# Range checks in halves behind the score transposes, reduced one step later, in an attention and two-layer FFN kernel

## The chip, the cores and the metric

The kernel runs on one core of a Trainium2 chip. The metric is the device time of one execution in microseconds (us). Before the change it is 730.16 us, the median of three runs (728.69 to 731.04).

The engines go by short names: PE is TensorE (PEld its weight loads), DVE VectorE, ACT ScalarE, POOL GpSimd, SP the engine that issues nearly all DMAs here. Each works through its own instructions in order and waits on semaphores for the others.

## What is computed

Attention over 4 batches, 8 heads, 768 positions and 64 dimensions, with a few global keys (`n_global` 8) and a local causal window (`n_local` 96), followed by two matrix products with an activation between them:

```python
scores = scale * np.matmul(q, k.transpose(0, 1, 3, 2)) + bias   # bias: -slope * distance
scores = np.where(keep, scores, -1000000000.0)                  # keep: global or local
a = np.exp(scores - np.max(scores, axis=-1, keepdims=True))
a = a / (np.sum(a, axis=-1, keepdims=True) + 1e-09)
x = np.matmul(a, v)                  # then heads side by side: 3072 tokens x 512
h = x @ w_in                         # 512 x 2048
g = np.where(h >= 1, h, np.where(h <= -1, 0.0, (h + 1) ** 2 / 4.0))
out = g @ w_out                      # 2048 x 512
```

q, k and v are float32; the two weight matrices arrive as float64.

## The kernel before

The 3072 tokens are 24 units of 128 (`UNITS`: batch and block; the first blocks of the four batches come first), and 12 chunks of two units. A unit's eight heads are handled in two halves of four. A half-unit n = 2 * unit + half goes through two functions:

- `attend`: score matmuls `s` (L295) into PSUM; on DVE bias and minimum (`z`, `nm`, L304); exponentials on ACT (L310); the probabilities `ph` as a float16 high part (ACT, L364) and low part (DVE, L365); and a DMA transpose `pt` of both, issued by SP (L369).
- `attend2`: output products `av` of `pt` with the values `vt` (L395); on DVE the division by the sum, giving `x` (L401); high and low parts `xh` (ACT L404, POOL L405); and a second DMA transpose, `xt` (L409).

The first block of a batch has versions without DMA transposes.

The FFN of a chunk is 8 calls of `ffn1` (24 matmuls L467, then ACT L475, DVE L479 and L480, ACT L483, POOL L484) and 8 of `ffn2` (12 matmuls each, L498). High and low parts of weights and activations take the place of float32 matmuls. `load` brings a unit's q, k and v; `load_v` (L246) loads a block of values into `vr`, a ring of three buffers, and splits it into `vt` on ACT (L214) and DVE (L216). `weight` loads and splits one 128-wide piece of a weight matrix.

The kernel is valid only for inputs within certain ranges. It therefore collects range data on the way, compares them at the end (L139 to L147, result `badi`), and takes a general path if a limit is broken. For this it reads inputs a second time:

- `check_weight(num, src)`, 32 of them: a 512 KB load of a weight piece into `c_raw` (L437), in the ring `stage` of three buffers, then two reduces on DVE (L443), largest and least magnitude, of 128 x 512 elements each.
- `check_qkv(num)`, 12 of them: a 512 KB load of values (`cqkv`, L277), then on ACT a square with an accumulated sum (L278).

The order is written by hand as a list of slots. A slot is one `ffn1` call or one `ffn2` call, and 16 slots make a chunk. Half-unit n's `attend` is traced at slot `first[n]` (4n - 16 - `LEAD`, so 4n - 23, from n = 12 on) and its `attend2` at `second[n]`, that is `first[n] + GAP`, at most `first[n + 2]`, and before its own chunk's slot; the loads `LDGAP` slots ahead of `attend`. From chunk `CK0` = 4 on, the checks are spread evenly over the slots up to the middle of chunk 11, weights first. A planner then lays out each engine's instructions: among those that are ready by its model of durations, the one traced first goes first. `tc.issue_after(ins)` makes what is traced under it, and runs on the engine of `ins`, come after `ins` in that engine's order; it adds no wait.

```python
        while c >= CK0 and checks and len(checks) > NCK - NCK * (slot + 1 - 16 * CK0) / (16 * (11.5 - CK0)):
            f, args = checks.pop(0)
            with tc.issue_after(late[-1].ins):
                f(*args)
```

`late` holds the `xt` transposes, which SP issues. So a check's load comes behind the latest `xt` on SP, and the reduces are placed by the planner alone.

## Time and profile before

| what | value |
|---|---|
| median of three runs | 730.16 us (728.69 to 731.04) |
| the profiled execution, its own time | 727.93 us |
| its span, first to last instruction | 726.2 us |
| DMA traffic | 97.40 MB, mean 134 GB/s |
| DVE reduces of the checks | 64 |
| squares of the value checks on ACT | 12 |

The profile is one execution. The page gives busy time, share of the span and number of instructions of each engine, then the chain of work that ended last, by line. Other views list waits (who waited for whom), a timeline (start, length, engine, line, operation, tiles, and in brackets the idle time before it and what ended it), groups of equal instructions, and busy time in chosen stretches. Matmuls overlap, so one lasts longer than the distance to the next. "SPq" is an instruction of SP's queue; for a DMA its length is the time to issue it, not to land.

### The profile page before, as it was taken

To read this page: it belongs to the slowest core of one execution; us is meant where nothing else is said; L and a number is where in the kernel's file an instruction comes from. 1 tells how busy PE (TensorE), PEld (TensorE's weight loads), DVE (VectorE), ACT (ScalarE), POOL (GpSimd) and SP (SyncE) were. 2 spreads that over 40 slices of the span, in tenths; PEclk is the share of its full clock that TensorE was granted. 3 is DMA by queue.
4 is the path that set the end of the run, shared out by engine and by line. 5 is a ranking of instruction groups with operands and counts; after the bars stand their busy time and mean duration, and the time that the engine had idled before them with its cause. 6 is when DMAs were issued, how large, how long until landed. Compare 5 with 4: busy or idle time off the path is not lost.

```text
span 726.2 us, 13000 instructions
## 1 busy us (share of the span) xinstructions
PE 647.0 (89%) x4912; PEld 434.0 (60%) x4912; DVE 418.5 (58%) x1023; ACT 358.4 (49%) x906; POOL 203.4 (28%) x200
## 2 busy tenths in 40 slices
PE   1787699999899999899997899898899799799995
PEld 1575577656756857646745755663674674475762
DVE  2678899764744744745843863654583674272240
ACT  1575578854634735524733553443552463473530
POOL 0222467432411422311420421240231141042130
PEclk9999799999999999999999899899899999999998
DMA  7544655567434456576466547546366445645301
GB/s 256 185 146 143 207 187 176 121 143 159 96 80 111 113 102 140 119 149 173 121 164 181 120 111 169 143 106 164 97 182 147 112 110 117 138 95 132 115 2 34
DMA packets 161191, 97.40 MB, mean 134 GB/s; under 512 B 116576, under 2 KB 145248, under 8 KB 161120
## 3 DMA queue, kind: packets, MB, share of 16 engines
q1 hardware_dynamic: 160256, 95.44, 51.7%
q10 hardware_dynamic: 864, 1.05, 0.4%
q8 instruction: 40, 0.66, 0.4%
q14 instruction: 31, 0.25, 0.1%
HBM read 63.97 MB, written 6.29 MB: 97 GB/s over the span
## 4 chain that ended last, share of the span: by engine, by line
PE 57%; DMA 15%; DVE 9%; issue 8%; ACT 4%; SPq 3%; POOL 3%; DVEq 0%; POOLq 0%; ACTq 0%
PE o L498 25%; PE h L467 22%; DMA pt<-ph 6%; PE s L295 5%; DMA c_raw<-in_moe_w_in_dram 4%; PE av L395 3%; DMA c_raw<-in_moe_w_out_dram 3%; ACT z L310 2%; POOL xh L405 2%; DVE sq L443 2%; SPq L409 1%; DVE w L479 1%; SPq L369 1%; DMA w_raw<-in_moe_w_in_dram 1%; DVE w L480 1%
## 5 line engine op out<-in xcount | busy, mean ns | idle before, releaser
L467 PE MATMUL h<-xt,wih 128*128 128x256 f16 x1536 | 267.2, 280 | 4.7 <-DVE w L479 4.7
L467 PE MATMUL h<-xt,wil 128*128 128x256 f16 x768 | 214.7, 280 | 0.0
L484 POOL TENSOR_TENSOR gl<-w,gh 128x512 f16<-128x512 f32 x96 | 121.4, 1270 | 239.4 <-ACT gh L483 230.9
L467 PEld LDWEIGHTS <-wih 128*128 128x128 f16 x1536 | 152.0, 100 | 37.1 <-issue 13.1
L310 ACT ACTIVATE z<-z,nm 128x256 f32<-128x256 f32 (+1 forms) x192 | 91.8, 479 | 139.1 <-DVE nm L304 139.1
L498 PE MATMUL o<-woh,gh 128*128 128x512 f16 x384 | 149.3, 389 | 1.4 <-ACT gh L483 1.4
L498 PE MATMUL o<-wol,gh 128*128 128x512 f16 x384 | 148.8, 388 | 0.0
L498 PE MATMUL o<-woh,gl 128*128 128x512 f16 x384 | 147.4, 387 | 0.0
L498 PEld LDWEIGHTS <-gh 128*128 128x128 f16 x768 | 74.1, 99 | 88.5 <-issue 11.1
L483 ACT ACTIVATE gh<-w 128x512 f16<-128x512 f32 x96 | 60.2, 627 | 92.6 <-DVE w L480 91.9
L479 DVE SCALAR_TENSOR_TENSOR w<-h,u 128x512 f32<-128x512 f32 x96 | 65.7, 684 | 54.6 <-ACT u L475 50.7
L443 DVE TENSOR_REDUCE sq<-c_raw 128x1 f32<-128x512 f32 x64 | 40.9, 680 | 86.1 <-DMA c_raw<-in_moe_w_in_dram 44.1
L304 DVE CUSTOM_DVE_ANT_0 z<-s,bias 128x256 f32<-128x256 f32 (+1 forms) x192 | 67.0, 395 | 34.3 <-PE s L295 34.1
L467 PEld LDWEIGHTS <-wil 128*128 128x128 f16 x768 | 77.1, 100 | 11.4 <-POOL wil L224 0.3
L475 ACT ACTIVATE u<-h,half 128x512 f32<-128x512 f32 x96 | 64.7, 674 | 26.3 <-PE h L467 26.2
L405 POOL TENSOR_TENSOR xh<-x,xh 128x256 f16<-128x256 f32 x40 | 36.9, 922 | 137.1 <-ACT xh L404 136.1
L480 DVE SCALAR_TENSOR_TENSOR w<-u,w 128x512 f32<-128x512 f32 x96 | 72.6, 756 | 1.9
L395 PE MATMUL av<-vt,pt 128*128 128x64 f16 x960 | 36.4, 197 | 35.6 <-DMA pt<-ph 30.6
L498 PEld LDWEIGHTS <-gl 128*128 128x128 f16 x384 | 38.1, 99 | 46.6 <-issue 4.0
L365 DVE SCALAR_TENSOR_TENSOR ph<-z,ph 128x1024 f16<-128x1024 f32 x40 | 51.8, 1296 | 22.7 <-ACT ph L364 21.7
L395 PEld LDWEIGHTS <-pt 128*128 128x128 f16 x960 | 32.7, 100 | 47.2 <-DMA pt<-ph 43.9
L295 PE MATMUL s<-kw,qr 64*128 64x256 f32 x320 | 52.7, 408 | 0.0
(75 smaller groups left out, 524.0 us busy)
## 6 DMA issues: line engine op xcount, KB each, us to landing
w_raw<-in_moe_w_in_dram SPq DMA_DIRECT2D x16, 512.0 KB, 4.3
w_raw<-in_moe_w_out_dram SPq DMA_DIRECT2D x16, 512.0 KB, 3.5
c_raw<-in_moe_w_in_dram SPq DMA_DIRECT2D x16, 512.0 KB, 4.5
c_raw<-in_moe_w_out_dram SPq DMA_DIRECT2D x16, 512.0 KB, 4.5
qr<-in_q_dram SPq DMA_DIRECT2D x24, 256.0 KB, 2.8
kw<-in_k_dram SPq DMA_DIRECT2D x24, 256.0 KB, 3.7
vr<-in_v_dram SPq DMA_DIRECT2D x24, 256.0 KB, 2.8
out_dram<-ob SPq DMA_DIRECT2D x24, 256.0 KB, 2.8
```

Source lines behind the costliest of these rows:

```text
L295: nc.tensor.matmul(pair[r][:, j, 0:n], qtile[u][rows, 2 * hf + j, :], kb[rows, 2 * hf + j, 0:n], start=True, stop=True,)
L304: nc.vector.tensor_tensor_reduce(out=z[:, hh, :], in0=pair[hh // 2][:, hh % 2, 0:n], in1=bias[:, 4 * hf + hh, base : base + n], scale=-0.1 ...
L310: nc.scalar.activation(z[:, hh, :], z[:, hh, :], AF.Exp, bias=nm[:, c0 + hh : c0 + hh + 1], scale=-1.0, accum_out=sums[:, c0 + hh : c0 + h ...
L395: nc.tensor.matmul(av[:, hh, :], pt[:, a, hh, kt, :], vt[:, c, h * D : (h + 1) * D], start=(n == 0), stop=(n == 3 * NT - 1),)
L443: nc.vector.tensor_reduce(sq[:, col : col + 1], top, axis=AX.XY, op=op, apply_absolute_value=True)
L467: nc.tensor.matmul(hp[:, e, :], w[:, dc, f], xt[:, hf, 2 * a + j, :], start=(n == 0), stop=(n == 3 * NDC - 1),)
L475: nc.scalar.activation(u, hpf, AF.Relu, bias=half, scale=2.0 / (SV * SW), accum_out=su[:, col : col + 1])
L479: nc.vector.scalar_tensor_tensor(w, hpf, 4.0 / (SV * SW), u, op0=ALU.mult, op1=ALU.max)
L480: nc.vector.scalar_tensor_tensor(w, u, 4.0, w, op0=ALU.min, op1=ALU.mult)
L483: nc.scalar.activation(gh, w, AF.Copy)
L484: (nc.gpsimd if GL == "p" else nc.vector).tensor_sub(gl, w, gh)
L498: nc.tensor.matmul(po, a[:, cs], w[:, f, :], start=(f == 0 and n == 0), stop=(f == NFC - 1 and n == 2))
```

## The change

The value checks are made where the values are loaded anyway: `load_v` squares `vr` in place on ACT after the split, with the sum accumulated, and `check_qkv` with its twelve loads is gone. So 32 checks, not 44, are spread over the same slots.

`check_weight` issues two loads of 256 KB, one for each half of a piece, into the ring `kraw` of three buffers, and only notes them in `loaded`. Their reduces, `reduce_weight`, two for each half over 256 elements, are traced when the next check's turn comes, behind the latest `x` on DVE (`last`). What is left over is traced after the last slot. `late` now holds the score transposes `pt` in place of `xt`, so that check loads come behind the latest `pt` on SP. `GAP` goes from 4 to 5: `attend2` is traced one slot later. At the end one small reduce joins the two halves' maxima, and the comparisons with limits are regrouped.

```diff
-NQKV = B * H * S * D // (8 * P * P)
+NQKV = NU
 W_MAX = NQKV
-W_MIN = W_MAX + 2 * NFC
-NSQ = W_MIN + 2 * NFC
+W_MIN = W_MAX + 4 * NFC
+NSQ = W_MIN + 4 * NFC
...
-GAP = 4
+GAP = 5
...
+    peak = cpool.tile([P, NFC], F32, name="peak")
+    maxes = sq[:, W_MAX + 2 * NFC : W_MIN].rearrange("p (a b) -> p a b", b=2)
+    nc.vector.tensor_reduce(peak, maxes, axis=AX.X, op=ALU.max)
...
         split(VENG(u), vt[:, 0, :], vt[:, 1, :], vr, SV)
+        nc.scalar.activation(vr, vr, AF.Square, scale=SV, accum_out=sq[:, b * NB + i : b * NB + i + 1])
...
-        nc.sync.dma_start_transpose(
+        late.append(nc.sync.dma_start_transpose(
             out=pt.rearrange("p a b c d -> p (a b c) d"), in_=ph.rearrange("p a b -> p (a b)")
-        )
+        ))
...
-        nc.vector.tensor_tensor(x, av, r.unsqueeze(2).to_broadcast([P, 4, D]), op=ALU.mult)
+        last.append(nc.vector.tensor_tensor(x, av, r.unsqueeze(2).to_broadcast([P, 4, D]), op=ALU.mult))
...
-        late.append(nc.sync.dma_start_transpose(
+        nc.sync.dma_start_transpose(
             out=xts[c][:, hf, :, t * P : (t + 1) * P], in_=xh.rearrange("p a b -> p (a b)")
-        ))
+        )
...
     def check_weight(num, src):
+        for e in range(2):
+            r = raw.tile([P, 2 * P, 2], I32, tag="kraw", name=f"c{num}_{e}_raw")
+            if num < NFC:
+                part, dst = src[:, 2 * e : 2 * e + 2], r.rearrange("p (a b) t -> p a (b t)", a=2)
+            else:
+                part, dst = src[:, 0, e * 2 * P : (e + 1) * 2 * P], r.rearrange("p b t -> p (b t)")
+            nc.sync.dma_start(dst, part.bitcast(I32))
+            top = r.bitcast(F32)[:, :, 1]
+            loaded.append((num, e, top))
+
+    def reduce_weight(num, e, top):
+            for col, op in ((W_MAX + 2 * num + e, ALU.max), (W_MIN + 2 * num + e, ALU.min)):
+                nc.vector.tensor_reduce(
+                    sq[:, col : col + 1], top, axis=AX.X, op=op, apply_absolute_value=True
+                )
...
-    checks = [(check_weight, w_args(n)[:2]) for n in range(2 * NFC)] + [(check_qkv, (n,)) for n in range(NQKV)]
+    checks = [(check_weight, w_args(n)[:2]) for n in range(2 * NFC)]
...
             f, args = checks.pop(0)
+            while loaded:
+                with tc.issue_after(last[-1].ins):
+                    reduce_weight(*loaded.pop(0))
             with tc.issue_after(late[-1].ins):
                 f(*args)
+    while loaded:
+        reduce_weight(*loaded.pop(0))
```

## The prediction

> **What bounds the kernel now.** The page first: its span, its busy shares and the chain that ended last.

> ```profile
> span 726.2 us, 13000 instructions
> ...
> PE 647.0 (89%) x4912; PEld 434.0 (60%) x4912; DVE 418.5 (58%) x1023; ACT 358.4 (49%) x906; POOL 203.4 (28%) x200
> ...
> PE o L498 25%; PE h L467 22%; DMA pt<-ph 6%; PE s L295 5%; DMA c_raw<-in_moe_w_in_dram 4%; PE av L395 3%; DMA c_raw<-in_moe_w_out_dram 3%; ACT z L310 2%; POOL xh L405 2%; DVE sq L443 2%; SPq L409 1%; DVE w L479 1%; SPq L369 1%; DMA w_raw<-in_moe_w_in_dram 1%; DVE w L480 1%
> ```

> TensorE has the most work, but the chain also runs through the check loads (`c_raw`, 4% and 3%) and the reduces on them (L443, 2%), work that no matmul reads. So the next view is busy time by stage: the start; a stage with attention and FFN but no checks yet; the same with checks, from the first check load (275 us) on; the last chunk without attention.

> ```profile
> 0.00:125.00 125.00, 93.69 (x541) 69.74 (x542) 96.80 (x257) 72.84 (x178) 47.57 (x53) 0.95 0.59 189
> ...
> 195.00:270.00 75.00, 74.79 (x594) 48.04 (x596) 38.09 (x96) 36.93 (x97) 19.06 (x19) 0.98 0.46 103
> 270.00:676.00 406.00, 367.84 (x2923) 242.23 (x2920) 225.43 (x534) 189.91 (x487) 101.08 (x95) 0.96 0.56 137
> 676.00:719.00 43.00, 42.61 (x293) 28.34 (x290) 12.16 (x21) 14.23 (x31) 9.96 (x9) 1.00 0.07 26
> ```

> The columns are the length, busy time of PE, PEld, DVE, ACT and POOL, granted clock, DMA share and GB/s. Without checks PE is idle for 0.2 of 75 us; with them for 406 - 367.8 = 38.2 us, at a clock of 0.96, which is another 406 x 0.04 = 16 us of lost matmul time. No other stage has anything like it. DVE is busy 55% there, so it isn't short of throughput. The waits of that stage (total, times, longest) say what it lacks:

> ```profile
> DVE sq L443 <- DMA c_raw<-in_moe_w_in_dram: 44.1, 13, 6.5
> DVE sq L443 <- DMA c_raw<-in_moe_w_out_dram: 41.8, 11, 9.3
> ...
> PE av L395 <- DMA pt<-ph: 28.5, 13, 3.8
> ...
> ACT cqkv L278 <- DMA cqkv<-in_v_dram: 26.1, 9, 5.1
> ...
> PE h L467 <- DVE w L479: 4.7, 2, 3.4
> ...
> PE av L395 <- DVE w L479: 3.9, 1, 3.9
> ...
> PE av L395 <- DVE nm L304: 0.7, 1, 0.7
> ```

> PE's four rows add up to 37.8 us in 17 gaps, all but 0.4 of the idle time: mostly the output products (`av`) waiting for transposed scores (`pt`). The two DVE rows are the cause: the reduces stand in DVE's order ahead of their data, and DVE, which works in order, stands still for 86 us. One check in the timeline:

> ```profile
> 386.53 0.38 PE L467 MATMUL h<-xt,wih 128*128 128x256 f16 x2
> ...
> 390.42 0.58 SPq L437 DMA_DIRECT2D c_raw<-in_moe_w_out_dram  x1
> ...
> 391.10 3.60 SPq L369 DMA_TRANSPOSE pt<-ph  x1
> ...
> 394.94 1.28 DVE L443 TENSOR_REDUCE sq<-c_raw 128x1 f32<-128x512 f32 x2 [4.35 <-DMA c_raw<-in_moe_w_out_dram]
> ...
> 396.78 0.88 PE L395 MATMUL av<-vt,pt 128*128 128x64 f16 x24 [3.78 <-DMA pt<-ph]
> ...
> 398.71 0.61 PE L467 MATMUL h<-xt,wih 128*128 128x256 f16 x2
> ```

> It costs three times. DVE idles 4.35 us, with softmax and FFN elementwise work behind it. The load stands just ahead of a score transpose, whose issue takes 3.60 us on SP. And after PE's gap a pair of matmuls takes 0.61 us, not 0.38. The transposes show the second cost in general; first the stage without checks, then the one with them:

> ```profile
> L369 SPq DMA_TRANSPOSE pt<-ph x6: 1317/1870/1978, 199.6 to 263.9; - x6
> ...
> DMA to landing us min/median/max: 4.2/4.3/6.0
> ```

> ```profile
> L369 SPq DMA_TRANSPOSE pt<-ph x27: 1761/3273/4740, 276.1 to 656.5; - x27
> ...
> DMA to landing us min/median/max: 4.2/5.5/7.2
> ```

> A median of 1.2 us more to landing. Order matters, not only traffic: a load behind the transpose doesn't hurt it. At 332.96 the issue takes 1.83 us though a load follows; at 321.11 it takes 3.78 us with a load 0.1 us ahead.

> ```profile
> 320.43 0.58 SPq L437 DMA_DIRECT2D c_raw<-in_moe_w_in_dram  x1
> 321.11 3.78 SPq L369 DMA_TRANSPOSE pt<-ph  x1
> ...
> 332.96 1.83 SPq L369 DMA_TRANSPOSE pt<-ph  x1
> 334.84 1.10 SPq L437 DMA_DIRECT2D c_raw<-in_moe_w_in_dram  x1
> ```

> **The change part by part.** Durations and the length of a group:

> ```profile
> L443 DVE TENSOR_REDUCE sq<-c_raw 128x1 f32<-128x512 f32 x64 | 40.9, 680 | 86.1 <-DMA c_raw<-in_moe_w_in_dram 44.1 <-DMA c_raw<-in_moe_w_out_dram 41.8
> ...
> L214 ACT ACTIVATE vt<-vr 128x512 f16<-128x512 f32 x24 | 14.6, 618 | 6.0 <-PE av L395 3.8 <-DMA vr<-in_v_dram 2.1
> ...
> L278 ACT ACTIVATE cqkv<-cqkv 128x1024 f32<-128x1024 f32 x12 | 12.7, 1055 | 27.9 <-DMA cqkv<-in_v_dram 27.9
> ...
> L278 ACT ACTIVATION_READ_ACCUMULATOR cqkv<-cqkv 128x1 f32 x12 | 2.2, 186 | 0.0
> ```

> ```profile
> c_raw<-in_moe_w_in_dram SPq DMA_DIRECT2D x16, 512.0 KB, 4.5
> ...
> vr<-in_v_dram SPq DMA_DIRECT2D x24, 256.0 KB, 2.8
> ```

> ```profile
> 227.01 5.24 PE h L467 x48
> ```

> A slot of the order is one group: 24 of these 48 matmuls, 2.6 us.

> 1. *Reduces one step on.* A check's reduces are now traced at the next check, 3.75 slots or 9.8 us later (before, 44 checks shared the 120 slots; now 32 do), and ordered behind an `x` on DVE. With check j at slot 64 + floor(3.75 j), half-unit n's scores at slot 4n - 23 and its output products at 4n - 18, I went through all 32. For 23 of them the reduces follow the `x` of the very half-unit whose `pt` stands ahead of the load, or a later one. That `x` needs `pt` landed (4.3 us after its issue began) and the products done; the load, issued when `pt`'s issue of 1.9 us is over, lands about 2.8 to 4.5 us after that, at about the same moment. There DVE's wait should go. For nine (j = 8 to 12, 24 to 27) the `x` is one half-unit earlier and doesn't protect the reduce. Checks cost 54.2 us (38.2 + 16) now, 1.7 each; the nine keep between 0 and 9 x 1.7 = 15 us. The mean gap is 38.2 / 17 = 2.2 us and part 3 gives 2.6 us more room, so I take a little over half: 8.

> 2. *Loads behind score transposes.* They no longer stand just ahead of `pt`, so its landing should go back towards 4.3 us. They now stand ahead of the output transposes (`xt`), needed only when the next chunk's FFN begins, six slots (16 us) after a chunk's last `av`. Cost there: none. The exception is chunk 2, whose last `av` moves to slot 29, three slots ahead of slot 32: 0 to +2.

> 3. *Output products one group on.* `av` comes five slots after its scores, not four: 2.6 us more for softmax, transpose and landing. This also covers the one gap without checks, at 195.2, and the slow clock behind it:

> ```profile
> 195.00:210.00 15.00, 14.80 (x127) 9.76 (x128) 7.82 (x20) 6.69 (x19) 4.13 (x4) 0.89 0.34 76
> ```

> With the gap of 2.1 us (its first 0.2 lies after 195) and 15 x 0.11 = 1.6 us of clock, -3.7.

> 4. *Halves.* 128 reduces of 256 elements take the place of 64 of 512. The trace has no such reduce. Bounds: 340 ns, half of 680, to 680. I take 410 (fixed part about 140), so 128 x 0.41 = 52 against 44 us of instruction time: 9 us more on DVE (0 to 44), over 310 us (120 slots) and more, in which it idles 45%: nothing on the path. SP issues 64 loads for 32, and two halves of 2.8 us against one of 4.5 add 1.1 us of transfer per check: hidden, since it lies ahead of need. In a ring of three buffers a check's second half waits for the reduces of the half three before it. What is queued behind that on SP are `xt`, the unit loads and the next `pt`.

> 5. *Values squared in place.* Twelve loads of 512 KB and twelve squares of 1.06 + 0.19 us go (15 us of ACT, 26 us of ACT waits; exponentials stood behind them). In come 24 squares of about 0.62 + 0.19, 19 us, each behind DVE's low half of the same tile, and the tile is released later by that much. Beside 49% busy ACT: 0. In the first 125 us, with some six squares while DVE is busy 97 us, they can cost 6 x 0.81 = 5 us; since a planner lays out the start anew around them, it can as well come out as much shorter: -4 to +5. Taken for this and chunk 2 together: +2.

> 6. *Tail.* The verdict on the checks comes before the last output rows are even copied:

> ```profile
> 709.33 0.15 DVE L147 CAST badi<-anybad 128x1 int32<-128x1 f32 x1 [7.29 <-POOL anybad L145]
> ```

> ```profile
> 718.64 0.60 ACT L503 ACTIVATE ob<-o 128x512 f32<-128x512 f32 x1 [9.76 <-PE o L498]
> ```

> 9 us of room for one more small reduce: 0.

> **Sum**, against the profiled execution's own 727.9 us (span 726.2): 727.9 - 38.2 - 16 - 3.7 + 8 + 2 = 680. The median shown, 730.2, lies 2.2 higher, so 682 on its scale. If every PE gap and slow stretch went and nothing came back, 727.9 - 57.9 + 2.2 = 672.

> **Rivals.**

> *The waits come back by half.* The order on each engine is planned with modelled durations, and that plan placed the reduces ahead of their data before. If it again does so for half of the checks, or DVE lateness only moves, half of 54 is kept: 727.9 - 27 - 3.7 + 2 + 2.2 = 701. For: 24 waits in 32 checks now. Against: the order behind `x`. 17 in 100.

> *The slow clock stays.* [...] 3 in 100. [...]

> *Nothing gained.* PE's gaps end in `pt`, not in a check; if the transposes are late of themselves, only part 3 helps, and other work takes up the room: 726 to 732. Against: 195:270, with the same transposes and no gap after its first. The same comes out if the planner lays the reduces back where they were. 5 in 100.

> *Slower: SP held by the ring of three.* The second half's load waits on SP for reduces, those for an `x`, that for a product. If the hold lasts longer than the 2.6 us of new room with the next `pt` behind it, each check costs more than now. A hold of one DVE wait of today (86 / 24 = 3.6 us) plus the 1.1 us of the second transfer is 2.1 us over that room; with 1 us of clock, 3.1 us for each of 32 checks, 99 us given back: 682 - 8 + 99 = 773; with half of the checks 724, and from 18 of them on slower than now. Against: the reduces of three halves back are traced before the load, and a chunk's `x` mostly comes before the next `pt`. 5 in 100.

> **How the numbers follow.** Forecast, waits of the checks nearly gone: 70 in 100, from 668 (no PE gap left, start 4 us shorter) to 692 (the nine at 15 us, the start at +5). Half kept: 17, around 701 and up to 713. The clock 3, nothing 5, slower 5. The range 668 to 709 holds the forecast, the clock and most of the half case. What this kernel's measurement can tell from no change is about 0.3%, 2.2 us. Faster by more: 70 + 17 + 3 and half of "nothing", 92. Within: 2. Slower: 6, the ring and the upper edge of "nothing".

> **What would show it.** Right: DVE's waits for `c_raw` below 20 us in total; PE idle below 12 us and clock at 0.98 or more between the first check and the last attention; `pt` landing at a median near 4.3 us; no `cqkv`; the stages before 125 us and after the last attention as long as now, within 3 us. Wrong: SP waiting at the check loads with `pt` behind them; reduces that still wait 3 us or more; a longer start from squares on ACT.

## The result, and the profile after

The changed kernel takes 675.43 us (median of four runs, 674.57 to 676.21) against 729.42 us before in the same session: a ratio of 0.926, interval 0.9235 to 0.9283. That is 54.0 us less; the prediction said 682, with 668 to 709 as its range.

The page of the profile after, its span, busy shares and chain:

```profile
span 673.3 us, 13132 instructions
...
PE 626.1 (93%) x4912; PEld 425.2 (63%) x4912; DVE 423.6 (63%) x1087; ACT 363.2 (54%) x930; POOL 198.8 (30%) x200
...
PE o L495 34%; PE h L464 33%; PE s L290 8%; PE av L390 4%; POOL gl L481 2%; DMA pt<-ph 1%; DMA w_raw<-in_moe_w_in_dram 1%; PE av L333 1%; POOL xh L400 1%; PE tp L324 1%; DMA kw<-in_k_dram 1%; DVE w_f L161 1%; DVE w_bits L160 1%; PE xtp L341 0%; DVE bias L209 0%
```

The check loads and the reduces have left these rows of the chain: it now runs through matmuls. DVE and ACT do 5 us more work each, in a shorter span. By stage (length, then busy time of PE, PEld, DVE, ACT, POOL, clock, DMA share, GB/s; the last attention now ends near 613 us):

```profile
195.00:270.00 75.00, 75.00 (x606) 47.75 (x605) 42.86 (x109) 42.61 (x115) 22.18 (x22) 1.00 0.51 111
270.00:635.00 365.00, 355.38 (x2999) 241.67 (x2997) 228.35 (x596) 191.99 (x496) 98.95 (x96) 1.00 0.56 137
635.00:667.00 32.00, 32.00 (x201) 19.32 (x198) 9.88 (x16) 7.71 (x17) 7.49 (x8) 1.00 0.03 10
```

PE's idle time in the stage with checks went from 38.2 to 9.6 us and the clock from 0.96 to 1.00. The waits, over the whole span for DVE and from 125 us on for PE:

```profile
DVE sq L440 <- DMA c_raw<-in_moe_w_in_dram: 19.2, 9, 5.2
DVE sq L440 <- DMA c_raw<-in_moe_w_out_dram: 19.0, 9, 5.0
```

```profile
PE av L390 <- DMA pt<-ph: 5.4, 4, 3.2
PE h L464 <- DVE w L476: 4.2, 3, 1.7
```

DVE's wait for check data fell from 85.9 to 38.2 us, not to nothing, and it isn't spread evenly. Two places of DVE's timeline in the changed kernel:

```profile
309.11 0.42 DVE L396 TENSOR_TENSOR x<-av,r 128x256 f32<-128x256 f32 x1
309.44 1.39 DVE L440 TENSOR_REDUCE sq<-c_raw 128x1 f32<-128x256 f32 x4
...
413.59 0.42 DVE L396 TENSOR_TENSOR x<-av,r 128x256 f32<-128x256 f32 x1
...
419.88 1.41 DVE L440 TENSOR_REDUCE sq<-c_raw 128x1 f32<-128x256 f32 x4 [4.96 <-DMA c_raw<-in_moe_w_out_dram]
421.21 0.41 DVE L299 CUSTOM_DVE_ANT_0 z<-s,bias 128x256 f32<-128x256 f32 x1
```

At 309 us the reduces follow an `x` and find their data landed. At 419.88 DVE has stood still for 4.96 us, and the softmax of the next scores (L299) comes after that. All 18 waits lie at checks 8 to 12 and 24 to 31. Nine of these (8 to 12, 24 to 27) are those whose `x` the prediction found one half-unit too early. The last four come at the end of attention, where no later `x` exists; no wait of PE follows them (its last is the 3.2 us at 612 us).

Where the time went, by the first FFN matmul of a chunk (the 192nd, 384th and so on of `h` in each trace):

| stretch | before | after | difference |
|---|---|---|---|
| up to chunk 2 | 173.7 | 174.8 | +1.1 |
| chunk 2 (holds the gap near 195 us) | 53.1 | 49.2 | -3.9 |
| chunk 3 | 49.5 | 49.2 | -0.3 |
| chunks 4 to 10 | 400.5 | 352.1 | -48.4 |
| chunk 11 to the last matmul | 41.8 | 41.8 | 0.0 |
| last matmul to the end of the span | 7.6 | 6.2 | -1.4 |

### The profile page after: what moved, and what is told of

Same layout as the page of the kernel before. It is cut to its first block, busy times and chain, and to the rows that moved or that the text cites. A ratio compares the mean times of both kernels' runs of the same rounds, so it can differ in the third digit from the quotient of the medians.

```text
span 673.3 us, 13132 instructions
## 1 busy us (share of the span) xinstructions
PE 626.1 (93%) x4912; PEld 425.2 (63%) x4912; DVE 423.6 (63%) x1087; ACT 363.2 (54%) x930; POOL 198.8 (30%) x200
## 4 chain that ended last, share of the span: by engine, by line
PE 80%; issue 7%; DVE 5%; DMA 3%; POOL 3%; ACT 1%; SPq 1%; POOLq 0%; DVEq 0%; ACTq 0%
PE o L495 34%; PE h L464 33%; PE s L290 8%; PE av L390 4%; POOL gl L481 2%; DMA pt<-ph 1%; DMA w_raw<-in_moe_w_in_dram 1%; PE av L333 1%; POOL xh L400 1%; PE tp L324 1%; DMA kw<-in_k_dram 1%; DVE w_f L161 1%; DVE w_bits L160 1%; PE xtp L341 0%; DVE bias L209 0%
## 5 line engine op out<-in xcount | busy, mean ns | idle before, releaser
L464 PE MATMUL h<-xt,wih 128*128 128x256 f16 x1536 | 258.5, 274 | 4.2 <-DVE w L476 4.2
L464 PE MATMUL h<-xt,wil 128*128 128x256 f16 x768 | 210.5, 274 | 0.0
L481 POOL TENSOR_TENSOR gl<-w,gh 128x512 f16<-128x512 f32 x96 | 119.3, 1248 | 188.1 <-ACT gh L480 173.8
L464 PEld LDWEIGHTS <-wih 128*128 128x128 f16 x1536 | 148.0, 98 | 32.9 <-issue 10.6
L495 PE MATMUL o<-woh,gh 128*128 128x512 f16 x384 | 147.1, 383 | 1.4 <-ACT gh L480 1.4
L480 ACT ACTIVATE gh<-w 128x512 f16<-128x512 f32 x96 | 60.1, 626 | 77.8 <-DVE w L477 77.4
L299 DVE CUSTOM_DVE_ANT_0 z<-s,bias 128x256 f32<-128x256 f32 (+1 forms) x192 | 67.3, 396 | 44.1 <-PE s L290 43.9
L477 DVE SCALAR_TENSOR_TENSOR w<-u,w 128x512 f32<-128x512 f32 x96 | 77.5, 808 | 1.5
L400 POOL TENSOR_TENSOR xh<-x,xh 128x256 f16<-128x256 f32 x40 | 34.4, 861 | 143.7 <-ACT xh L399 141.4
L440 DVE TENSOR_REDUCE sq<-c_raw 128x1 f32<-128x256 f32 x128 | 46.1, 412 | 38.4 <-DMA c_raw<-in_moe_w_in_dram 19.2
L495 PEld LDWEIGHTS <-gl 128*128 128x128 f16 x384 | 37.8, 99 | 46.1 <-issue 1.7
L290 PE MATMUL s<-kw,qr 64*128 64x256 f32 x320 | 48.7, 402 | 0.0
L359 ACT ACTIVATE ph<-z 128x1024 f16<-128x1024 f32 x40 | 42.0, 1050 | 0.6
## 6 DMA issues: line engine op xcount, KB each, us to landing
w_raw<-in_moe_w_in_dram SPq DMA_DIRECT2D x16, 512.0 KB, 4.5
w_raw<-in_moe_w_out_dram SPq DMA_DIRECT2D x16, 512.0 KB, 3.4
c_raw<-in_moe_w_in_dram SPq DMA_DIRECT2D x32, 256.0 KB, 3.2
c_raw<-in_moe_w_out_dram SPq DMA_DIRECT2D x32, 256.0 KB, 3.3
qr<-in_q_dram SPq DMA_DIRECT2D x24, 256.0 KB, 3.3
kw<-in_k_dram SPq DMA_DIRECT2D x24, 256.0 KB, 4.4
vr<-in_v_dram SPq DMA_DIRECT2D x24, 256.0 KB, 3.5
out_dram<-ob SPq DMA_DIRECT2D x24, 256.0 KB, 2.7
```

Of the source, the lines that this page charges most:

```text
L290: nc.tensor.matmul(pair[r][:, j, 0:n], qtile[u][rows, 2 * hf + j, :], kb[rows, 2 * hf + j, 0:n], start=True, stop=True,)
L299: nc.vector.tensor_tensor_reduce(out=z[:, hh, :], in0=pair[hh // 2][:, hh % 2, 0:n], in1=bias[:, 4 * hf + hh, base : base + n], scale=-0.1 ...
L464: nc.tensor.matmul(hp[:, e, :], w[:, dc, f], xt[:, hf, 2 * a + j, :], start=(n == 0), stop=(n == 3 * NDC - 1),)
L477: nc.vector.scalar_tensor_tensor(w, u, 4.0, w, op0=ALU.min, op1=ALU.mult)
L480: nc.scalar.activation(gh, w, AF.Copy)
L481: (nc.gpsimd if GL == "p" else nc.vector).tensor_sub(gl, w, gh)
```

## The experiments

Ratios are to the kernel before, timed beside each run on the same chip. Differences to the changed kernel are between medians of separate sessions; taken from the ratios they come out up to 3 us different. Theory A is that of the prediction: the time was lost because reduces stood on DVE ahead of their data. Rival B puts the gain down to SP's order (loads no longer ahead of score transposes), rival C to the extra group of room, rival D to the smaller loads.

### One part undone in the changed kernel

**undo_step**: the reduces are traced with their own loads.

```diff
             f, args = checks.pop(0)
-            while loaded:
-                with tc.issue_after(last[-1].ins):
-                    reduce_weight(*loaded.pop(0))
             with tc.issue_after(late[-1].ins):
                 f(*args)
+            while loaded:
+                reduce_weight(*loaded.pop(0))
```

> The changed kernel (675.4 us) with one part undone: a check's reduces are traced with its own loads again, with no order behind x. Theory A, the reduces standing on DVE ahead of their data are the main cost: DVE waits for c_raw come back to over 70 us in total (38.2 now), PE idles 15 to 35 us between 270 us and the last attention, and the time is 695 to 715 us; the loads behind the score transposes and the extra group keep the rest. Rival B, the gain came from the loads leaving the place ahead of the score transposes: at most 682 us. Rival C, the gain came from the extra group of room for the output products: at most 685 us, the DVE waits coming back without a price.

Measured: 719.75 us, 0.986 of before (0.9816 to 0.9911). DVE's and PE's waits:

```profile
DVE sq L440 <- DMA c_raw<-in_moe_w_out_dram: 57.8, 21, 6.9
DVE sq L440 <- DMA c_raw<-in_moe_w_in_dram: 53.4, 19, 6.6
```

```profile
PE av L390 <- DMA pt<-ph: 22.8, 12, 4.0
PE h L464 <- DVE w L476: 18.8, 13, 2.6
```

DVE waits are 111 us and PE gaps 41.6 us, and 44 of the 54 us are lost, although the loads still stand behind the score transposes and the extra group is still there. B and C can't explain this.

**undo_behind**: the check loads go behind the output transposes again (`late` collects `xt` and not `pt`).

```diff
-        late.append(nc.sync.dma_start_transpose(
+        nc.sync.dma_start_transpose(
             out=pt.rearrange("p a b c d -> p (a b c) d"), in_=ph.rearrange("p a b -> p (a b)")
-        ))
+        )
...
-        nc.sync.dma_start_transpose(
+        late.append(nc.sync.dma_start_transpose(
             out=xts[c][:, hf, :, t * P : (t + 1) * P], in_=xh.rearrange("p a b -> p (a b)")
-        )
+        ))
```

> The changed kernel with the check loads ordered behind the output transposes again, which puts them ahead of score transposes. Theory A: the median landing of pt goes from 4.3 back towards 5.5 us, the extra group covers most of that, DVE waits stay under 50 us, time 675 to 686 us. Rival B: 700 us or more. Rival C: below 680 us.

Measured: 666.61 us, 0.913 (0.9085 to 0.9169). It is 9 us faster than the changed kernel. Neither A nor B had that. C's bound, below 680 us, holds it, but C names nothing in the place of the loads that would gain time. DVE's waits and the transposes' landing (from 195 to 640 us):

```profile
DVE sq L440 <- DMA c_raw<-in_moe_w_in_dram: 9.5, 4, 4.9
...
DVE sq L440 <- DMA c_raw<-in_moe_w_out_dram: 1.7, 3, 1.0
```

```profile
DMA to landing us min/median/max: 4.3/4.3/6.4
```

`pt` lands as early as in the changed kernel (median 4.3 us), and DVE waits 11.2 us instead of 38.2. By the trace, the first reduce on a half starts a median of 4.4 us after its data has landed, against 2.8 us in the changed kernel: the loads run earlier against their reduces. The prediction's slot rule, applied to loads behind `xt`, gives the reason: a check is unprotected when no newer `x` is traced by the next check's turn, and before the end of attention that is so at checks 8 and 24 alone, not at nine. The trace's seven waits lie at checks 8, 24, 29, 30 and 31. So putting the loads behind `pt` cost 9 us, by theory A's own mechanism. What it was to avoid had become small by other parts: only 9 of 40 transposes have a check load that was issued less than 2.5 us before them (14 before the change), and these land in a median of 4.7 us, with half loads ahead, where whole loads in the kernel before made it 5.6.

**undo_gap** is `GAP = 4`. **undo_halves** has whole loads of 512 KB in the ring `stage` and two reduces of 512 elements for each check, one step on as before:

```diff
...
-        for e in range(2):
-            r = raw.tile([P, 2 * P, 2], I32, tag="kraw", name=f"c{num}_{e}_raw")
...
-            loaded.append((num, e, top))
+        r = stage.tile([P, *n, 2], I32, tag="raw", name=f"c{num}_raw")
+        nc.sync.dma_start(r.rearrange("p a b t -> p a (b t)"), src.bitcast(I32))
+        loaded.append((num, r.bitcast(F32)[:, :, :, 1]))
...
```

> The changed kernel with GAP 4: output products one group earlier again. Theory A: softmax and transposes are on time without DVE waits, as they were in the stage without checks; only the nine checks whose reduces come too early, and the one gap at 195 us, show: 680 to 692 us. Rival B: below 682 us. Rival C: 710 us or more, with PE gaps before most of the output products.

> The changed kernel with whole check loads of 512 KB in the old ring of three and two reduces of 512 elements for each check, still one step on. Theory A: what counts is when the reduces run, not their size: 672 to 681 us, DVE 9 us less busy in the reduces, DVE waits of 30 to 50 us. Rival D, halves keep the queue and DVE free for shorter times, and that is part of the gain: 685 us or more.

Measured: undo_gap 681.94 us, 0.934 (0.9296 to 0.9376): 6.5 us slower than the changed kernel. That is inside A's range, but not by A's reasoning, which kept the nine early checks: with `GAP` 4 every `x` is traced one slot sooner, and by the slot rule only check 12 is early. DVE waits 12.4 us, not 38.2. What PE loses, 14.4 us in 11 gaps, is all at output products that wait for `pt`, which is C's part. So the run takes away room and protects the checks at once. undo_halves 683.24 us, 0.935 (0.9312 to 0.9394): 7.8 us slower, between the bounds of A and of D. Loads land in a median of 4.6 us instead of 3.3, DVE waits 40.6 us, PE gaps are 15.3 us.

**undo_square**: the twelve second reads of values are back (the function `check_qkv` and its twelve calls at the end of the list), the squares on loaded tiles gone.

```diff
...
-        nc.scalar.activation(vr, vr, AF.Square, scale=SV, accum_out=sq[:, b * NB + i : b * NB + i + 1])
...
-    checks = [(check_weight, w_args(n)[:2]) for n in range(2 * NFC)]
+    checks = [(check_weight, w_args(n)[:2]) for n in range(2 * NFC)] + [(check_qkv, (n,)) for n in range(NQKV)]
```

> The changed kernel with values read again in twelve loads of 512 KB and squared on ACT, in place of the squares on the loaded tiles; so 44 checks share the slots and the weight checks stand closer. Theory A: ACT waits of 20 us or more for these loads, exponentials behind them, and other checks meeting the wrong slots: 677 to 692 us. If the second reading cost nothing: 672 to 677 us.

Measured: 696.10 us, 0.951 (0.9468 to 0.9555), 20.7 us slower than the changed kernel, more than expected. ACT waits 24.8 us for the value loads. But the weight checks, now every 2.7 slots, also meet worse places: by the slot rule 18 of 32 have an `x` one half-unit early, and DVE waits 57.0 us. The run can't split the two.

### One part done alone in the kernel before

**only_step** traces the reduces at the next check's turn, behind the latest `x`; all else is as before. **only_gap** is `GAP = 5` alone.

```diff
...
+            while loaded:
+                with tc.issue_after(last[-1].ins):
+                    reduce_weight(*loaded.pop(0))
             with tc.issue_after(late[-1].ins):
                 f(*args)
...
```

> The kernel before with one part done: reduces traced at the next check's turn, behind the latest x; whole loads behind the output transposes, GAP 4, the value checks reading again. Theory A: at least half of the gain, 685 to 705 us, DVE waits for c_raw under 40 us; what remains are the value loads that ACT waits for, and late score transposes. Rival B: above 715 us. Rival C: above 715 us.

> The kernel before with GAP 5 alone. Theory A: DVE waits for c_raw stay above 70 us; the extra 2.6 us take part of the gaps at the output products, not those of the FFN behind DVE: 705 to 724 us. Rival C: below 695 us.

Measured: only_step 691.33 us, 0.948 (0.9428 to 0.953): about 39 of the 54 us come from this part alone, as A had it, where B and C had above 715 us. DVE waits 33.8 us, and ACT still waits 27.1 us for value loads. only_gap 736.65 us, 1.0075 (1.0045 to 1.0106): slower by about 5 us, where A had 6 to 25 us less and C more than that. Its waits for checks and on PE:

```profile
DVE sq L443 <- DMA c_raw<-in_moe_w_in_dram: 55.1, 13, 9.0
DVE sq L443 <- DMA c_raw<-in_moe_w_out_dram: 45.7, 10, 7.4
```

```profile
PE av L395 <- DMA pt<-ph: 32.4, 13, 4.6
PE h L467 <- DVE w L479: 17.2, 10, 2.9
```

With the planner laying the order out anew, DVE waits 101 us instead of 86, and the gaps at the FFN go from 4.7 to 17.2 us. A was right that DVE's waits stay, and wrong that the extra group gains anything beside them: the gaps at the output products stay too (32.4 us). C is out as the main cause.

### The place of the checks against the half-units

**aligned** runs a check at every fourth slot just after a half-unit's output products are traced, so that each check's reduces follow the `x` of the half-unit whose `pt` stands ahead of its load. **misaligned** is one slot earlier, so that the first 28 have the `x` of the half-unit before (the last four come after attention's last `pt`). **no_checks** leaves the 32 weight checks out, their columns filled with a constant.

```diff
-        while c >= CK0 and checks and len(checks) > NCK - NCK * (slot + 1 - 16 * CK0) / (16 * (11.5 - CK0)):
+        if slot >= 58 and slot % 4 == 2 and checks:
```

(misaligned: `slot >= 57 and slot % 4 == 1`)

> The changed kernel with one line altered: a check at every fourth slot, 58, 62, ... 182, just after the output products of a half-unit are traced, so that each check's reduces follow the x of the half-unit whose score transpose stands ahead of its load. Theory A: the waits at nine checks go; DVE waits for c_raw under 10 us, no PE gap over 1 us after 125 us, 665 to 670 us. If the remaining gaps have another cause (rival B or C, or plain lateness of transposes): 673 to 678 us.

> The same one slot earlier: checks at 57, 61, ... 181, just before the output products are traced, so that all 32 checks' reduces follow the x of the half-unit before and nothing but the planner's own durations holds them back. Theory A: all checks behave as the nine did; DVE waits for c_raw of 80 to 140 us, PE gaps of 15 to 30 us, 685 to 705 us. Rivals B and C, to which this order on DVE is indifferent: 673 to 678 us.

> The changed kernel without the 32 weight checks: their loads and reduces are left out and their columns filled with a constant. The floor for this change. Theory A: 664 to 669 us; the weight checks of the changed kernel then cost 7 to 11 us. A floor of 674 us or more would say that what idles at the end has nothing to do with checks.

Measured: aligned 663.48 us, 0.910 (0.9054 to 0.9153); misaligned 700.93, 0.964 (0.9574 to 0.9695); no_checks 662.90, 0.909 (0.9041 to 0.9137). The stretch from 270 to 600 us, first of aligned, then of misaligned:

```profile
270.00:600.00 330.00, 330.00 (x2813) 226.76 (x2812) 215.38 (x564) 186.67 (x484) 94.52 (x93) 1.00 0.57 141
```

```profile
270.00:600.00 330.00, 308.69 (x2572) 207.67 (x2571) 197.78 (x509) 169.86 (x445) 90.81 (x83) 0.99 0.55 130
```

DVE's waits for check data, aligned (270 to 640 us) and misaligned (the whole span):

```profile
DVE sq L440 <- DMA c_raw<-in_moe_w_in_dram: 3.5, 2, 2.0
DVE sq L440 <- DMA c_raw<-in_moe_w_out_dram: 1.7, 2, 1.1
```

```profile
DVE sq L440 <- DMA c_raw<-in_moe_w_in_dram: 68.7, 19, 6.3
...
DVE sq L440 <- DMA c_raw<-in_moe_w_out_dram: 38.4, 18, 5.4
```

The same loads and the same reduces, one slot apart: PE idles 0.0 us of the stretch in the one and 21.3 in the other; DVE waits 5.2 us and 107.1 us. aligned and no_checks came out 1 to 2 us below what A had for them. In aligned all 32 checks together cost nothing that can be measured against none at all (0.6 us, the intervals overlap). This is the most direct evidence for A, and aligned beats both kernels: 66.7 us less than before.

### Whether halves and the fifth group are still needed then

**aligned_whole** is undo_halves with the slots of aligned; **aligned_gap4** is aligned with `GAP = 4` and the slots one earlier (57, 61, ...), since the output products are.

> Whole loads of 512 KB and reduces of 512 elements as in undo_halves, with a check at every fourth slot as in aligned. undo_halves was 7.8 us slower than the changed kernel. Theory A, a longer landing (4.5 us for 3.3) hurts only where a reduce comes before its data: with the order protected it costs nothing, 662 to 667 us, DVE waits under 12 us. Rival D, halves are worth something in themselves: 669 us or more.

> GAP 4 with checks at every fourth slot right after the output products (57, 61, ..., since these are traced one slot earlier), so that every reduce follows the x of its load's half-unit. Theory A: once DVE doesn't wait, four groups are room enough but for the gap near 195 us, as in the stage without checks before: 665 to 671 us, PE gaps after 270 us under 5 us. Rival C, the fifth group itself is needed because scores, softmax and transpose take longer than four groups: 674 us or more, with PE gaps at many output products.

Measured: aligned_whole 668.12 us, 0.914 (0.9097 to 0.9185), between the two expectations: 4.6 us slower than aligned by the medians, 2.8 by the ratios, whose intervals overlap, so that the times alone don't show a price of whole loads. In the traces chunks 4 to 10 take 345.5 us, against 341.1 in aligned. DVE waits only 3.6 us there. The largest of its four PE gaps, 1.9 us at 543.93, is a score transpose that was ready at 534.8 and was issued at 537.8, behind an output transpose that SP had to wait for. Whether whole loads or another order by the planner made this one late stays open.

aligned_gap4 680.10 us, 0.929 (0.9249 to 0.9335): here A was wrong and C right. DVE waits 6.3 us for checks, yet eight output products after 270 us wait for their transposes:

```profile
PE av L390 <- DMA pt<-ph: 11.7, 8, 2.1
```

Seven of the eight are the first half-unit of a chunk's last unit (numbers 22, 26, 30 and so on to 46), six of these with 1.5 to 2.1 us each. For number 22, at 296.87 us, scores end at 281.8 and `pt` lands at 296.8: 15.1 us. In aligned the same half-unit takes 12.7 us (278.2 to 290.9), and its product is due 14.9 us after the scores, so there is room. Four groups were enough in the stage without checks (195 to 270 us before), but with nothing to spare. In aligned_gap4 DVE is busy from 280.8 us until half-unit 22's probabilities are done at 292.5, but for 0.5 us, and 1.5 us of that are reduces. That the reduces alone use up the room isn't shown: no run has four groups and no checks.

## Why the prediction was right

The total was right, and so was its main step, part 1. Three others (parts 2, 3 and 4) were wrong by sign or size, some in the kernel's favour and one against it; that these partly cancel is luck.

- *DVE waits behind PE's gaps* (part 1): shown. Undoing the step loses 44 us, doing it alone gives 39, and one slot of shift between aligned and misaligned makes 37.
- *What there is to remove*: said 54.2 us in the stage with checks. By aligned, whose chunks 4 to 10 take 341.1 us as do those of no_checks, it was 400.5 - 341.1 = 59.4. The gap and clock rows account for 54 to 55 of it; the rest stands in neither.
- *Nine checks keep a part*, said 8 us: they were found in the trace where the slot rule put them, and 352.1 - 341.1 = 11.0 us remain. Mechanism right, size 3 us low; the upper bound of 15 held. 59.4 less 11.0 is the -48.4 of the table, against -46.2 predicted.
- *Loads behind score transposes* (part 2): wrong. The step said that loads would no longer delay `pt` and that this costs nothing. `pt` does land in 4.3 us, but undo_behind has that as well, and is 9 us faster. The step priced the load's place only for what stands behind it on SP; it overlooked that a later load is later for its own reduces, which part 1 depends on. The sum does hold this cost, as the 8 us of the nine checks, but the prediction didn't see that parts 2 and 3 together make the nine: without part 2 two checks are early, without part 3 one.
- *One group on* (part 3): -3.7 us for the gap near 195 us was right (-3.9). The sum gives it no saving of its own beyond this, and that was wrong: in the changed kernel it is worth 6.5 us in all (5.6 by the ratios), and next to well-placed checks 16.6 (13.8). The two sizes differ because the fifth group also turns eight more checks early: aligned_gap4 is only 1.8 us faster than undo_gap, aligned 12.0 us faster than the changed kernel. Alone the group costs 5 us or so, which the prediction didn't consider.
- *Halves* (part 4): "nothing on the path" was wrong by 7 to 8 us in the changed kernel (undo_halves), in its favour; with well-placed checks the price of whole loads lies between nothing and 5 us. The reduce of 256 elements was priced right: 0.41 us, beside 0.68 us for 512 before (a straight line through the two gives the fixed part of 0.14). Here it is in the tile view of the changed kernel, with the loads' landing (before: 4.5):

```profile
L440 DVE TENSOR_REDUCE sq<-c_raw x128: 406/410/421, 284.1 to 625.2; 128x1 f32<-128x256 f32 x128
...
DMA to landing us min/median/max: 2.7/3.3/5.0
```

- *Values squared in place* (part 5): the squares' own price of 0 is consistent with the start (+1.1 us, said +2 with chunk 2; over all runs this stretch takes 173.1 to 175.1 us with the squares and 172.5 to 174.9 without) and with a stage without idle time in aligned. That the twelve loads they replace cost PE time was part of the 54.2 and is borne out by undo_square, though not in size.
- *The slow clock*: 0.96 to 1.00, as the sum had it. The rival that it stays slow, 3 in 100 by the author's estimate, is out.
- *SP held by the ring of three*: hardly. SP waits at check loads for reduces 2.3 us in all, at most 0.8 at once. Of the chain, SP's queue is 1%.
- *The tail*: 1.4 us shorter, not foreseen. only_step and only_gap don't have it (7.4 and 7.3 us), every run built on the changed kernel does (5.9 to 6.2); its cause stays open.

The signs named in advance came out so: no `cqkv`, `pt` at 4.3 us, PE idle 9.6 us (below 12), clock 1.00. DVE's waits were to be under 20 us and are 38, at the places named, and one sign of being wrong came too: seven reduces wait 3 us or more, all at the nine checks.

## What to carry to other kernels

DVE worked in order here and paid for a waiting reduce with what stood behind it: at 419.88 us it stood still for 4.96 us, and the softmax of the next scores came after that. Work that nothing waits for, such as a check, should be put where its data is certain to have landed, tied to an event on the same engine that can't come earlier, and the distance should be checked for every instance: a period of 3.75 slots against one of 4 left nine of 32 unprotected, and a period of 4 made all 32 nearly free in one phase and cost 38 us one slot away from it. The distance also changes when something else moves: here the loads' place and the extra group, each of which the prediction took to be free, made the nine together. Parts of a change aren't additive: more room alone made this kernel slower, and is worth 14 to 17 us once the waits are gone.

## What the runs showed of the hardware

The length of a PE gap alone doesn't decide whether the clock falls. Before, 195:210 follows a gap of 2.1 us and has a clock of 0.89; after the change a gap of 3.2 us leaves it at 1.00:

```profile
612.03 0.88 PE L390 MATMUL av<-vt,pt 128*128 128x64 f16 x24 [3.21 <-DMA pt<-ph]
```

```profile
600.00:615.00 15.00, 11.79 (x79) 5.81 (x78) 9.68 (x25) 6.44 (x17) 5.38 (x4) 1.00 0.39 98
615.00:630.00 15.00, 15.00 (x93) 8.84 (x92) 7.49 (x23) 2.28 (x5) 0.67 (x1) 1.00 0.55 167
```

On SP, a DMA transpose with a check load just ahead of it took longer in these runs, and the more so behind the larger load. Medians of issue and landing over the `pt` transposes: 1.9 and 4.3 us with no check load issued in the 2.5 us before (26 in the kernel before, and all 40 in the changed kernel); 3.0 and 4.7 us behind loads of 256 KB (undo_behind, nine transposes); 3.6 and 5.6 us behind 512 KB (the kernel before, 14 transposes, value loads counted too).
